# Weight conversion in an attention, FFT-mixing and gating kernel: temporaries moved to PSUM, the second weight's lower parts moved to VectorE

## The chip, the cores and the metric

The kernel runs on one core of a Trainium2 chip. The metric is the device time of one execution in microseconds (us). An engine takes its instructions in a fixed order; the engines are PE (TensorE: matmuls and transposes), DVE (VectorE), ACT (ScalarE), POOL (GpSimd) and SP (SyncE, which here only issues transfers). SBUF is the on-chip work memory, PSUM the smaller one into which PE writes; a full tile of it here is 128 partitions by 512 fp32 values, called a bank. GpSimd is given no operand in PSUM in this kernel.

## What is computed

The inputs are batches of 2, 8 heads, 768 positions, 64 values a head, all in fp32, and the weights, which come as fp64. Cut to what matters:

```
q_bucket, k_bucket = signs of q @ proj and k @ proj, as numbers     # 6 bits
scores = where(q_bucket == k_bucket, q @ k.T / 8, -1e9)
x = softmax(scores) @ v                          # [2, 768, 512] over all heads
u = x + real(fft(fft(x, axis=1), axis=2))
un = (u - mean(u)) / sqrt(var(u) + 1e-6)
y = u + relu(un @ w_ch1) @ w_ch2                 # 512 -> 2048 -> 512
gate = sigmoid(causal convolution of y over 5 positions)
out = (gate * (y @ w_val)) @ w_out
```

## The kernel before, in words

Matmuls run in fp16. Each operand is split into an upper part (its rounding to fp16) and a lower part (what is left), and a product is made of three matmuls: upper by upper, lower by upper, upper by lower. So every activation and every weight needs two elementwise steps, one for each part.

Weights are fp64 in device memory. `weights` (L414) loads a block into a ring of slots in SBUF and converts it in pieces. `widen` (L408) makes fp32 out of the two 32-bit halves by three instructions of VectorE: L410 (shift and mask of the high half into the temporary `wt`), L411 (sign and exponent bits, from ring and `wt` into `wt`), L412 (low bits, from ring and `wt` into `wt`). `split` (L128) then makes the two parts. Its last argument is a word of letters: with two letters, the first engine makes the upper part with the scale in the same instruction (`copy_of`, L112 on ScalarE) and the second the lower part, on VectorE by one instruction that scales and subtracts (`rest_of`, L126). With three letters, the first engine scales the temporary in place (L112 on ScalarE, L114 on GpSimd), the second makes the upper part and the third subtracts (L120). The words of the three sets of weights stand in `HOW`; a set with several words takes them in turn.

- First stretch, up to about 175 us: attention of batch 0 (`a0`), and beside it the first 1536 columns of `w_ch1`, 12 pieces of 128x512, word `av`. The temporaries are two buffers in the SBUF pool `tmp`. The loop at L953 steps through the attention's 38 remaining steps and makes one conversion after each step that `STEP` picks: before, every third (0, 3, 6 up to 33). `last` (L430) keeps a conversion's `widen` behind the newest score reduction on VectorE.
- Middle stretch, about 175 to 365 us: mixing of batch 0 (its FFT as matmuls, VectorE's sums on tile `z`), its norm, attention of batch 1 (`a1`) and the first feed-forward, and beside them the last 512 columns of `w_ch1` and all of `w_ch2`, 40 pieces of 128x256, word `aag`, temporaries in two buffers of the SBUF pool `wst`. `GATES` ties five of these pieces behind marks of other work.
- Late weights, 425 to 475 us: `w_val` and `w_out`, 8 pieces of 128x512, words `av`, `gag`, `av` in turn (three pieces with `gag`), temporaries in the SBUF pool `late`. Beside them runs the mixing of batch 1; after that the remaining feed-forwards and the gating, most of it PE.

The attention works in pairs of two score tiles (`pair`, L312): PE makes the scores (L320), VectorE their maximum (L330), ScalarE the exponential (L333) and the upper part (L112), GpSimd the lower part (L120), SyncE issues the transposing transfer (`at<-a`, L346), and PE multiplies by the values (`unit_out`, L355). `prep` (L230) splits q and k of the next group, transposes them (`tb<-st`, L247), and makes the hash products into a PSUM tile of the pool `pools.bt`, which has one buffer (L259), from which VectorE takes the signs (L264). Twice per `prep` that buffer is filled and read. Mixing's first matmuls (`zp`) and the norm's use the same pool.

All loads and transposes are issued by SyncE, in one order: a load that waits for its ring slot holds up the transposes behind it. The order of each engine's instructions is planned when the kernel is built, by a simulation of the instructions' times, which moves later work ahead into free places as far as data, buffers and the ties written by hand allow.

Of the kernel before, what the change touches and what calls it, by code (L numbers as in the profile page):

```python
# [9 lines left out]
INT32 = mybir.dt.int32  # L10
# [32 lines left out]
FLY = ('g', 'g')  # L43
CONV = "vvvv", "vvvv"
OO = ('aa', 'aa')
HOW = (('av',), ('aag',), ('av', 'gag', 'av'))
LEFT = 512
WB = 512
QW = {None: "s", "w2": "s"}
# [4 lines left out]
LO = {(1, 4, 0): 'v'}  # L54
NPRE = 0
PACE = 1
STEP = 3
W0 = 0
EARLY = (0, 'prep', 1)
UO = 'aa'  # L60
PREN = '-g'
# [16 lines left out]
def attention_fft_mix_gated_kernel(  # L78
# [49 lines left out]
    def split(h, l, i, s, how):  # L128

        unit = isinstance(s, float) and s == 1.0  # L130
        if len(how) == 3:
            if not unit:
                copy_of(i, i, s, how[0])
            s, unit, how = 1.0, True, how[1:]
        copy_of(h, i, s, how[0])
        if unit:
            return both(l, i, h, ALU.subtract, how[1])
        return rest_of(l, h, i, s, how[1])
# [18 lines left out]
    @contextmanager  # L157
    def after_mark(ins):
        with ExitStack() as stack:
            for i in ins:  # L160
                stack.enter_context(tc.issue_after(i))
            yield


    class Pool:
# [8 lines left out]
        def widen(self, stack, bufs):  # L174
            self.more, self.extra = stack.enter_context(tc.tile_pool(name="q_" + self.name, bufs=bufs, reuse_waits="tile", **self.kw)), bufs
            stack.callback(self.narrow)
# [237 lines left out]
    def weights(blocks, ring, pool, how, wp=WP, name=None, pre=()):  # L414

        n, m, at, rest = len(ring), len(pre), {}, list(enumerate(blocks))

        def load(done):
            while rest:
                i, (src, _, _, _) = rest[0]  # L420
                if i >= max(m, done) + n:
                    return
                at[i] = pre[i] if i < m else ring[(i - m) % n]
                nc.sync.dma_start(out=at[i], in_=src)
                rest.pop(0)

        load(0)
        yield
        for i, (src, h, l, s) in enumerate(blocks):
            r = at[i].rearrange("p (n x) -> p n x", x=2)  # L430
            for c in range(0, r.shape[1], wp):
                cl = slice(c, c + wp)
                t = pool.tile([128, wp], INT32, tag="wt", name="wt", bufs=2)
                k = (name, i * (r.shape[1] // wp) + c // wp)
                with after_mark([marks[GATES[k]]] if k in GATES else last if PACE and not name else []):
                    marks[k] = widen(t, r[:, cl, 0], r[:, cl, 1], t).ins
                split(h[:, cl], l[:, cl], t.bitcast(FP32), s, how[k[1] % len(how)])
                if cl.stop < r.shape[1]:
                    yield
            load(i + 1)  # L440
            yield

    def slots(t):
        return [t[:, i] for i in range(t.shape[1])]

    def w_blocks(src, dst, s, width, c0=0, c1=None):
        rows, cols = src.shape
        for c in range(c0, c1 or cols, width):
            for r in range(rows // 128):
                cl = slice(c, c + width)  # L450
                yield src[r * 128:(r + 1) * 128, cl].bitcast(INT32), dst[:, 0, r, cl], dst[:, 1, r, cl], s
# [425 lines left out]
    def drain(gen):  # L877
        for _ in gen:
            pass

    if True:
        base = ctx.enter_context(ExitStack())
        pools = AttnPools(base, ld=2, ta=2, tb=1, vt=2, e=2, a=3, at=2, sm=4, sc=2, pv=1, bt=1)
# [4 lines left out]
        tmp = att.enter_context(tc.tile_pool(name="tmp", reuse_waits="tile", bufs=1))  # L888
# [20 lines left out]
        wp = pools.pv.tile([128, 512], FP32, tag="pv", name="wp")  # L909
# [27 lines left out]
        with tc.issue_after(marks[EARLY]):  # L937
            nc.sync.dma_start(out=cf, in_=dft_f)
            nc.sync.dma_start(out=cs, in_=dft_s)
            nc.sync.dma_start(  # L940
                out=cwd.rearrange("p c j x -> p c (j x)"), in_=conv_t.bitcast(INT32).rearrange("(c p) j -> p c j", p=128)
            )
            w = weights(
                list(w_blocks(w_ch1, w1, W1S, WB, 0, DFF - LEFT)),
                slots(work.tile([128, 2048 // WB, 2 * WB], INT32, tag="big", name="ring")),
                tmp,
                HOW[0],
                W1P,
                pre=[work.tile([128, 4 * WP], INT32, tag="t4", name="pre", bufs=4) for _ in range(NPRE)],
            )  # L950
            next(w)
        widen(cw, cwd[:, :, :, 0], cwd[:, :, :, 1], cwt)
        for i, _ in enumerate(a0):  # L953
            if (i % STEP == W0 % STEP and i >= W0) if PACE else i % 4:
                next(w, None)
            if i in (A1LD, A1AT):
                next(a1)
        for _ in w:
            pass
        att.close()  # L960
        w2 = ctx.enter_context(tc.tile_pool(name="w2p", reuse_waits="tile", bufs=1)).tile([128, 2, NF, DM], FP16, name="w2")
        gen_p = ctx.enter_context(tc.tile_pool(name="gen", reuse_waits="tile", bufs=2, space=PSUM))
        wst = base.enter_context(tc.tile_pool(name="wst", reuse_waits="tile", bufs=1))
        w = weights(
            list(w_blocks(w_ch1, w1, W1S, WP, DFF - LEFT)) + list(w_blocks(w_ch2, w2, W2S, WP)), slots(wst.tile([128, 2, 2 * WP], INT32, name="ring2")), wst, HOW[1], name="w2"
        )
# [9 lines left out]
        if F0FIRST:  # L976
# [3 lines left out]
        late = ctx.enter_context(tc.tile_pool(name="late", bufs=1, side="right", reuse_waits="tile"))  # L980
        lps = ctx.enter_context(tc.tile_pool(name="lps", side="right", reuse_waits="tile", bufs=2, space=PSUM))
        lps2 = ctx.enter_context(tc.tile_pool(name="lps2", side="right", reuse_waits="tile", bufs=4, space=PSUM))
        wv = late.tile([128, 2, KC, DM], FP16, name="wv")
        wo = late.tile([128, 2, KC, DM], FP16, name="wo")
        w = weights(
            list(w_blocks(w_val, wv, WVS, DM)) + list(w_blocks(w_out, wo, WOS, DM)),
            [late.tile([128, 2 * DM], INT32, tag=t, name="ring3") for t in ("x2", "gt", "gv")],
            late,
            HOW[2],
            WLP,  # L990
        )
# [102 lines left out]
```

## Time and profile before

| what | value |
|---|---|
| median of 3 runs | 707.6 us (707.6 to 710.81) |
| the profiled execution | 703.61 us |
| its span, first to last instruction | 701.8 us |
| VectorE busy | 534.5 us (76%) |
| PE busy | 572.9 us (82%) |
| ScalarE busy | 350.9 us (50%) |
| GpSimd busy | 313.2 us (45%) |

The span is the time from the first to the last instruction on the core; the execution's own time is 1.8 us longer. In a group's row, L120 is a line of the kernel, then come engine, operation, out<-in by the program's tiles, shapes and count; behind the bar the busy time in us and the mean duration of one in ns, and behind the next bar how long the engine had stood idle just before, with what ended that. A queue's name carries a q (SPq). The granted clock (PEclk) is TensorE's, as a share of full speed.

### The profile page before, as it was taken

Reading aid. Unit: us, or ns where it says so; the run is one execution under the profiler, and the core shown is the slowest. Engines: PE = TensorE matmul, PEld = TensorE weight load, DVE = VectorE, ACT = ScalarE, POOL = GpSimd, SP = SyncE. Lnnn points to the kernel's source line nnn. Section 1 sums busy time; section 2 is a strip of 40 time slices with the busy share of each in tenths; the row PEclk is TensorE's granted clock in tenths of the full one; section 3 lists DMA queues with packets and bytes.
Section 4 is the critical chain, followed back from the end, with each engine's and each line's share of the span. In section 5 each row is a group of like instructions: output and inputs, shape, how many; then the busy total and the mean of one; then the engine's idle time right before and its main releaser. Section 6 shows DMA issues by size and latency. Waiting matters only on the chain.

```text
span 701.8 us, 12761 instructions
## 1 busy us (share of the span) xinstructions
PE 572.9 (82%) x4958; PEld 436.3 (62%) x4958; DVE 534.5 (76%) x1002; ACT 350.9 (50%) x731; POOL 313.2 (45%) x321
## 2 busy tenths in 40 slices
PE   5775576666664769988789999799989999999997
PEld 2334353444343547666567789678767788888864
DVE  5799797997999998999875629996799346182582
ACT  4576767883866445776578725321434302121142
POOL 5665959795577722876556431455232100000000
PEclk8557878868975799999989999999999999999999
DMA  3989999999578552676875884200000000000001
GB/s 118 203 233 222 238 236 223 215 221 204 139 151 179 135 144 65 146 165 148 163 133 109 157 159 151 91 1 2 0 31 31 32 1 1 1 2 1 1 31 61
DMA packets 191804, 79.72 MB, mean 114 GB/s; under 512 B 176384, under 2 KB 182144, under 8 KB 191744
## 3 DMA queue, kind: packets, MB, share of 16 engines
q1 hardware_dynamic: 191168, 78.81, 50.6%
q8 instruction: 39, 0.64, 0.4%
q10 hardware_dynamic: 576, 0.10, 0.1%
q14 instruction: 21, 0.17, 0.1%
HBM read 32.50 MB, written 3.15 MB: 51 GB/s over the span
## 4 chain that ended last, share of the span: by engine, by line
PE 33%; DVE 27%; DMA 6%; issue 5%; POOL 4%; ACT 2%; SPq 1%; ACTq 0%; DVEq 0%; POOLq 0%
PE f L720 12%; PE f L703 10%; DMA at<-a 3%; DVE wt L412 3%; PE pv L355 2%; DVE sc L330 2%; DVE wt L411 2%; DVE wt L410 2%; DVE gt L745 2%; PE op L864 2%; POOL a L120 2%; DVE z L120 2%; DMA ring<-in_moe_w_ch_dram 2%; DVE h L685 1%; PE vp L839 1%
## 5 line engine op out<-in xcount | busy, mean ns | idle before, releaser
L120 POOL TENSOR_TENSOR a<-e,a 128x384 f16<-128x384 f32 x184 | 183.5, 1021 | 90.6 <-ACT a L112 50.6
L703 PE MATMUL f<-un,w 128*128 128x256 f16 x1152 | 134.6, 274 | 5.0 <-DVE h L685 4.7
L720 PE MATMUL f<-h,w 128*128 128x256 f16 x1152 | 132.3, 273 | 0.9 <-POOL w L120 0.9
L703 PEld LDWEIGHTS <-w 128*128 128x128 f16 x1152 | 112.7, 98 | 24.0 <-issue 7.2
L720 PEld LDWEIGHTS <-w 128*128 128x128 f16 x1152 | 111.5, 98 | 16.2 <-POOL w L120 1.4
L355 PE MATMUL pv<-at,vt 128*64 128x256 f16 x864 | 77.7, 335 | 31.3 <-DMA at<-a 21.0
L330 DVE TENSOR_SCALAR_CACHE_REDUCE sc<-sc 128x768 f32<-128x768 f32 x96 | 91.4, 961 | 14.4 <-PE sc L320 13.2
L355 PEld LDWEIGHTS <-vt 128*64 128x64 f16 x864 | 62.0, 136 | 56.4 <-issue 38.7
L333 ACT ACTIVATE e<-sc,mx 128x768 f32<-128x768 f32 x96 | 85.5, 891 | 4.1 <-POOL a L120 1.2
L320 PE MATMUL sc<-ta 96*128 96x384 f16 x192 | 54.4, 367 | 39.0 <-ACT e L333 28.6
L112 ACT ACTIVATE a<-e 128x768 f16<-128x768 f32 x96 | 79.9, 839 | 11.1 <-DMA at<-a 7.9
L685 DVE SCALAR_TENSOR_TENSOR h<-f,h 128x512 f16<-128x512 f32 x48 | 32.6, 684 | 34.4 <-ACT h L684 34.2
L320 PE MATMUL sc<-tb 128*128 128x384 f16 x192 | 56.1, 376 | 0.0
L684 ACT ACTIVATE h<-f 128x512 f16<-128x512 f32 x48 | 28.4, 591 | 49.2 <-PE f L703 49.0
L320 PEld LDWEIGHTS <-ta 96*128 96x128 f16 x192 | 17.5, 103 | 56.3 <-issue 42.0
L120 POOL TENSOR_TENSOR w<-wt,w 128x256 f16<-128x256 f32 x40 | 36.1, 910 | 32.6 <-ACT w L112 32.4
L112 ACT ACTIVATE x<-xb 128x256 f16<-128x256 f32 x24 | 11.8, 534 | 67.3 <-DVE xb L691 66.9
L331 ACT ACTIVATE mx<-mx 128x1 f32<-128x1 f32 x96 | 18.8, 197 | 52.7 <-DVE sc L330 48.1
L412 DVE SCALAR_TENSOR_TENSOR wt<-ring,wt 128x256 int32<-128x256 int32 (+1 forms) x60 | 43.3, 728 | 0.4
L691 DVE SCALAR_TENSOR_TENSOR xb<-f,xb 128x256 f32<-128x256 f32 x24 | 13.7, 615 | 37.6 <-PE f L720 37.6
L411 DVE SCALAR_TENSOR_TENSOR wt<-ring,wt 128x256 int32<-128x256 int32 (+1 forms) x60 | 41.3, 696 | 0.5
L812 DVE SCALAR_TENSOR_TENSOR gt<-xb,cw,gt 128x256 f32<-128x256 f32 x60 | 37.1, 673 | 0.0
(144 smaller groups left out, 905.5 us busy)
## 6 DMA issues: line engine op xcount, KB each, us to landing
ring<-in_moe_w_ch_dram SPq DMA_DIRECT2D x40, 256.0 KB, 3.0
ring<-in_moe_w_ch_dram SPq DMA_DIRECT2D x12, 512.0 KB, 4.4
lv<-in_v_dram SPq DMA_DIRECT2D x8, 384.0 KB, 3.7
out_dram<-ob SPq DMA_DIRECT2D x12, 256.0 KB, 2.0
lq<-in_q_dram SPq DMA_DIRECT2D x7, 384.0 KB, 3.8
lk<-in_k_dram SPq DMA_DIRECT2D x7, 384.0 KB, 4.2
ring<-in_moe_w_val_dram SPq DMA_DIRECT2D x4, 512.0 KB, 4.2
ring<-in_moe_w_out_dram SPq DMA_DIRECT2D x4, 512.0 KB, 3.5
```

Of the source, the lines that this page charges most:

```text
L112: return nc.scalar.activation(out=o, in_=i, func=ACTF.Copy, scale=s)
L120: return (nc.gpsimd if eng == "g" else nc.vector).tensor_tensor(out=o, in0=i0, in1=i1, op=op)
L320: nc.tensor.matmul(out=s[:, n, 0:384], lhsT=z[0:rows, 0, hh, r], rhs=z[0:rows, 1, hh, n * 384:n * 384 + 384], start=(x == 0), stop=(x == 1),)
L330: last[:] = [nc.vector.tensor_scalar(s, s, -(PEN * PEN) / 2, None, ALU.max, ALU.max, accum_out=m[:, 0:1]).ins]
L333: marks["first", 2 + j] = nc.scalar.activation(out=e.rearrange("p (a b) -> p a b", a=2), in_=s, func=ACTF.Exp, bias=m[:, 1:2], scale=SC, a ...
L355: nc.tensor.matmul(out=p[64 * hh:64 * hh + 64, :], lhsT=va[g][:, hh, c, x, :], rhs=at[hh][:, :, y, c, :], start=(c == 0 and n == 0), stop= ...
L411: nc.vector.scalar_tensor_tensor(out=tmp, in0=hi, scalar=-0x40000000, in1=tmp, op0=ALU.bitwise_and, op1=ALU.bitwise_or)
L412: return nc.vector.scalar_tensor_tensor(out=dst, in0=lo, scalar=29, in1=tmp, op0=ALU.logical_shift_right, op1=ALU.bitwise_or)
L685: nc.vector.scalar_tensor_tensor(out=h[:, 1, f:f + 2, :], in0=p, scalar=0.0, in1=h[:, 0, f:f + 2, :], op0=ALU.max, op1=ALU.subtract)
L703: nc.tensor.matmul(out=p[:, o, :], lhsT=w1[:, i, kd, (f + o) * 128:(f + o) * 128 + 128], rhs=un[:, j, kd, :], start=(k == 0), stop=(k == 3 ...
L720: nc.tensor.matmul(out=p[:, o, :], lhsT=w2[:, i, f, (d + o) * 128:(d + o) * 128 + 128], rhs=h[:, j, f, :], start=(k == 0), stop=(k == 3 * ...
L812: nc.vector.scalar_tensor_tensor(out=o, in0=src, scalar=cw[:, d, j:j + 1].bitcast(FP32), in1=o, op0=ALU.mult, op1=ALU.add)
```

## The change

Four things change. (1) `HOW`: the 40 pieces of the middle stretch go from `aag` to `av`, so that ScalarE makes the upper part with the scale in one instruction and VectorE makes the lower part; the three late pieces with `gag` become `av` as well. (2) The temporary `wt` of the first stretch is a whole PSUM bank from `pools.bt`, the pool with one buffer that the hash products use; that of the late weights is a bank of `lps2`, with four buffers. The middle stretch keeps its two buffers in SBUF. (3) The pacing of the first stretch: the 12 conversions follow steps 0, 3, 6, 8, 11, 13, 16, 19, 21, 24, 26 and 29. (4) `drain(w)` stands for the loop that did the same.

```diff
--- before.py
+++ after.py
@@ -43,7 +43,7 @@
 FLY = ('g', 'g')
 CONV = "vvvv", "vvvv"
 OO = ('aa', 'aa')
-HOW = (('av',), ('aag',), ('av', 'gag', 'av'))
+HOW = (('av',), ('av',), ('av',))
 LEFT = 512
 WB = 512
 QW = {None: "s", "w2": "s"}
@@ -54,8 +54,7 @@
 LO = {(1, 4, 0): 'v'}
 NPRE = 0
 PACE = 1
-STEP = 3
-W0 = 0
+STEP = 31
 EARLY = (0, 'prep', 1)
 UO = 'aa'
 PREN = '-g'
@@ -430,7 +429,7 @@
             r = at[i].rearrange("p (n x) -> p n x", x=2)
             for c in range(0, r.shape[1], wp):
                 cl = slice(c, c + wp)
-                t = pool.tile([128, wp], INT32, tag="wt", name="wt", bufs=2)
+                t = pool.tile([128, 512], INT32, tag="g", name="wt")[:, 0:wp] if name != "w2" else pool.tile([128, wp], INT32, tag="wt", name="wt", bufs=2)
                 k = (name, i * (r.shape[1] // wp) + c // wp)
                 with after_mark([marks[GATES[k]]] if k in GATES else last if PACE and not name else []):
                     marks[k] = widen(t, r[:, cl, 0], r[:, cl, 1], t).ins
@@ -943,7 +942,7 @@
             w = weights(
                 list(w_blocks(w_ch1, w1, W1S, WB, 0, DFF - LEFT)),
                 slots(work.tile([128, 2048 // WB, 2 * WB], INT32, tag="big", name="ring")),
-                tmp,
+                pools.bt,
                 HOW[0],
                 W1P,
                 pre=[work.tile([128, 4 * WP], INT32, tag="t4", name="pre", bufs=4) for _ in range(NPRE)],
@@ -951,12 +950,11 @@
             next(w)
         widen(cw, cwd[:, :, :, 0], cwd[:, :, :, 1], cwt)
         for i, _ in enumerate(a0):
-            if (i % STEP == W0 % STEP and i >= W0) if PACE else i % 4:
+            if i * 12 // STEP != (i - 1) * 12 // STEP and i < STEP:
                 next(w, None)
             if i in (A1LD, A1AT):
                 next(a1)
-        for _ in w:
-            pass
+        drain(w)
         att.close()
         w2 = ctx.enter_context(tc.tile_pool(name="w2p", reuse_waits="tile", bufs=1)).tile([128, 2, NF, DM], FP16, name="w2")
         gen_p = ctx.enter_context(tc.tile_pool(name="gen", reuse_waits="tile", bufs=2, space=PSUM))
@@ -985,7 +983,7 @@
         w = weights(
             list(w_blocks(w_val, wv, WVS, DM)) + list(w_blocks(w_out, wo, WOS, DM)),
             [late.tile([128, 2 * DM], INT32, tag=t, name="ring3") for t in ("x2", "gt", "gv")],
-            late,
+            lps2,
             HOW[2],
             WLP,
         )
```

## Rows read from the trace of the kernel before

**Rows 1.** Windows, length, busy PE, PEld, DVE, ACT, POOL, PEclk, DMA share, GB/s
```profile
50.00:175.00 125.00, 81.30 (x715) 54.92 (x715) 109.05 (x174) 87.98 (x189) 91.92 (x86) 0.79 1.09 221
175.00:350.00 175.00, 128.50 (x1131) 93.62 (x1128) 163.54 (x319) 107.83 (x240) 108.79 (x112) 0.88 0.63 143
350.00:425.00 75.00, 69.85 (x678) 56.46 (x677) 40.51 (x81) 47.76 (x104) 34.23 (x38) 0.95 0.76 150
425.00:475.00 50.00, 43.66 (x432) 38.37 (x430) 48.15 (x95) 19.88 (x28) 19.36 (x19) 1.00 0.19 62
475.00:700.00 225.00, 217.42 (x1875) 179.43 (x1872) 136.59 (x273) 60.05 (x113) 27.34 (x20) 1.00 0.04 15
```

**Rows 2.** Timeline of SyncE's queue, 30 to 180 us: start, duration
```profile
35.51 9.82 SPq L346 DMA_TRANSPOSE at<-a  x1
50.05 0.33 SPq L424 DMA_DIRECT2D ring<-in_moe_w_ch_dram  x1
...
160.90 12.31 SPq L346 DMA_TRANSPOSE at<-a  x3
173.26 1.05 SPq L424 DMA_DIRECT2D ring<-in_moe_w_ch_dram  x2
```

**Rows 3.** Timeline of VectorE, 43 to 54 us
```profile
43.42 1.02 DVE L410 TENSOR_SCALAR wt<-ring 128x512 int32<-128x512 int32 x1
...
46.05 0.42 DVE L410 TENSOR_SCALAR wt<-ring 128x512 int32<-128x512 int32 x1
46.39 0.68 DVE L411 SCALAR_TENSOR_TENSOR wt<-ring,wt 128x512 int32<-128x512 int32 x1
...
48.62 1.40 DVE L412 SCALAR_TENSOR_TENSOR wt<-ring,wt 128x512 int32<-128x512 int32 x1
...
52.30 1.22 DVE L126 SCALAR_TENSOR_TENSOR w<-wt,w 128x512 f16<-128x512 f32 x1
```

**Rows 4.** VectorE by form, 40 to 160 us: busy, mean ns, idle
```profile
L412 DVE SCALAR_TENSOR_TENSOR wt<-ring,wt 128x512 int32<-128x512 int32 x12 | 12.9, 1073 | 0.1
L126 DVE SCALAR_TENSOR_TENSOR w<-wt,w 128x512 f16<-128x512 f32 x12 | 12.7, 1067 | 2.0 <-ACT w L112 2.0
L411 DVE SCALAR_TENSOR_TENSOR wt<-ring,wt 128x512 int32<-128x512 int32 x12 | 12.0, 1000 | 0.1
L410 DVE TENSOR_SCALAR wt<-ring 128x512 int32<-128x512 int32 x12 | 7.9, 654 | 0.1
```

**Rows 5.** Groups of VectorE by form, 175 to 365 us
```profile
L412 DVE SCALAR_TENSOR_TENSOR wt<-ring,wt 128x256 int32<-128x256 int32 x40 | 24.6, 625 | 0.3
L411 DVE SCALAR_TENSOR_TENSOR wt<-ring,wt 128x256 int32<-128x256 int32 x40 | 23.9, 606 | 0.3
L410 DVE TENSOR_SCALAR wt<-ring 128x256 int32<-128x256 int32 x40 | 19.3, 486 | 3.7 <-DMA ring<-in_moe_w_ch_dram 3.0 <-POOL w L120 0.6
...
L685 DVE SCALAR_TENSOR_TENSOR h<-f,h 128x512 f16<-128x512 f32 x8 | 5.5, 683 | 0.4 <-ACT h L684 0.3
```

**Rows 6.** Tile wt, 40 to 160 us: min/median/max ns, starts
```profile
L126 DVE SCALAR_TENSOR_TENSOR w<-wt,w x12: 679/1146/1400, 52.3 to 151.4; 128x512 f16<-128x512 f32 x12
```

**Rows 7.** Tile wt, 175 to 365 us
```profile
L410 DVE TENSOR_SCALAR wt<-ring x40: 275/294/1709, 176.3 to 352.8; 128x256 int32<-128x256 int32 x40
...
L412 DVE SCALAR_TENSOR_TENSOR wt<-ring,wt x40: 390/421/1137, 179.0 to 357.6; 128x256 int32<-128x256 int32 x40
...
L120 POOL TENSOR_TENSOR w<-wt,w x40: 662/672/5902, 185.0 to 362.4; 128x256 f16<-128x256 f32 x40
```

**Rows 8.** Groups of GpSimd by form, 175 to 350 us
```profile
L120 POOL TENSOR_TENSOR w<-wt,w 128x256 f16<-128x256 f32 x38 | 34.7, 923 | 30.2 <-ACT w L112 30.1
```

**Rows 9.** Waits of SyncE's queue, 175 to 350 us: total, times, longest
```profile
SPq L346 <- POOL w L120: 30.8, 9, 4.0
```

**Rows 10.** Tile wt, 425 to 475 us
```profile
L410 DVE TENSOR_SCALAR wt<-ring x8: 408/420/833, 427.1 to 455.5; 128x512 int32<-128x512 int32 x8
...
L126 DVE SCALAR_TENSOR_TENSOR wv<-wt,wv x3: 683/690/1130, 434.4 to 443.1; 128x512 f16<-128x512 f32 x3
```

## The prediction

> **What bounds the kernel now.** I read the stretches first, then the queue that issues the transfers, then the groups of VectorE and GpSimd in each stretch. The rows to look at are those in which one column fills the stretch [rows 1].
>
> From 50 to 175 us it is the transfers. VectorE works 109 of 125 us, GpSimd 92, ScalarE 88, PE 81, and the sixteen DMA engines show a share of 1.09 [rows 1]. The queue itself shows why: SyncE issues one transfer behind the other, a transpose holding it for some 4 us (three in 12.31), until the first load for the next stage at 173.26 [rows 2]; 25 transposes and 17 plain loads follow each other there with at most half a microsecond between two. The one hole is at the start: the issue begun at 35.51 ends at 45.33, the next load goes at 50.05, and the VectorE instruction that frees its slot, L412 begun at 48.62 for 1.40 us, ends at 50.02 [rows 2, 3].
>
> From 175 to 350 us it is VectorE: 163.5 of 175 us busy, PE 128.5, ScalarE 107.8, GpSimd 108.8 [rows 1]. Mixing of batch 0, attention of batch 1 and forty conversions of weights share that engine. From 350 us on PE is short of nothing for long (69.9 of 75, 43.7 of 50, 217.4 of 225), so what comes late at 350 comes late at the end; only from 425 to 475 is VectorE full too (48.2 of 50) [rows 1].
>
> One property of the rows carries the argument. A VectorE instruction with two inputs in SBUF has no fixed price. L412 on 128x512 takes 1073 ns on the mean in the first stretch [rows 4] and can take 680 (one of the interleaved ones did in about that: L411 at 46.39, 0.68 us) [rows 3]. L685, which takes one input from PSUM and one from SBUF at the same size, has a mean of 683 ns in the middle of a stretch where GpSimd is 62% busy [rows 1, 5]. So what stretches the first kind and leaves the second alone goes with GpSimd's reading of SBUF.
>
> **First stretch: temporaries in PSUM, one buffer, new pacing.** Twelve conversions of 128x512 cost VectorE 654 + 1000 + 1073 + 1067 = 3794 ns each, 45.5 us [rows 4]. After the change L411, L412 and L126 read the temporary from PSUM; I price them like L685, 683 ns [rows 5]. L410 writes PSUM; no row shows that form. Bounds: 0.42 us, its quickest in this program [rows 3], and 0.68 us, the price of L685 at the same size. I take 0.68. Sum 4 x 0.68 = 2.73, 12 x 2.73 = 32.8 us, so VectorE works 12.7 us less.
>
> The Trainium skill, VectorE: DVE Perf Modes, section Why PSUM operands drop a tier, speaks against the change here: an operand in PSUM takes the two-port rate from such an instruction. By it L410 goes to the upper bound, by the row of before it would stay at the lower; the sum differs by 12 x 0.26 = 3 us of VectorE's time, which is hidden either way.
>
> Of the 12.7 us nearly nothing reaches the end: VectorE has 16 us free in this stretch as it is [rows 1], and SyncE's queue covers it [rows 2]. What can be gained is the hole of 4.7 us. With one buffer the second conversion can't be woven into the first, so its L410 (0.42) and L411 (0.68) no longer stand ahead of the first one's L412, which itself falls from 1.40 to 0.68, and its L410 from 1.02 [rows 3]: 0.42 + 0.68 + 0.72 + 0.34 = 2.2 us. I take **-2 us** (ends -4.7 and, if the single buffer holds things up, +8, see below). The new pacing moves conversions by at most four steps. The last one began its L126 at 151.4 us [rows 6], and the queue sets the stretch's end at 173: nothing, covered by the queue. Without that cover the same VectorE work would only stand elsewhere in the stretch, and its worst is one conversion, 2.7 us, in front of something urgent.
>
> **Middle stretch: VectorE takes over the lower parts.** Per conversion, 40 times: one ScalarE scaling goes (ScalarE is 62% busy, off the path, nothing), one GpSimd subtraction goes, median 672 ns, mean 923 [rows 7, 8], and one VectorE L126 on 128x256 comes, with both inputs in SBUF (this temporary is not moved to PSUM). Its nearest rows are L412 and L411 of the same size and stretch: median 421 ns, the undisturbed price, and mean 625 [rows 5, 7]. GpSimd is busy 62% of the stretch; without the 34.7 us of these subtractions [rows 8] 108.8 - 34.7 = 74 of 175, 42%. If the surcharge of 204 ns shrinks with that share, the new instruction costs 421 + 204 x 42/62 = 559 ns, 40 x 559 = 22.4 us (ends 16.8 and 25.0).
>
> The same shrinking gives time back. L412: (625 - 421) x 20/62 = 66 ns; L411: (606 - 421) x 20/62 = 60; L410: (486 - 294) x 20/62 = 62; together 188 ns x 40 = 7.5 us [rows 5, 7] (for L411 the median of L412, the form being the same). For the fewer other instructions with two inputs in SBUF I allow 1.5. Net on VectorE: 22.4 - 9 = +13.4 us, in a stretch where it has 11.5 idle [rows 1]. Those holes are where data were late; a longer queue fills some of them. I let half of them absorb: **+8 us** (ends: -6, if GpSimd's instructions cost VectorE their whole length, see below, and +16, nothing absorbed and the dear price).
>
> SyncE's transposes wait 30.8 us in this stretch for a GpSimd `w` [rows 9]. That wait goes, but the engine that makes their data is full, so the next wait is for the same conversions' L412 or for the scores on VectorE. Nothing; at most 3 us. Behind each new L126 stands everything else of VectorE's queue, the score reductions of attention 1 first, and ScalarE's exponentials wait for those; L126 also waits for ScalarE's upper part. Twelve such in the first stretch lost 2.0 us in all, 0.17 each [rows 4]; at that rate 40 lose 6.7, which is within the upper end.
>
> **Late weights.** Eight conversions of 128x512. Their temporaries in PSUM cost L410 the step from 0.42 to 0.68, 8 x 0.26 = 2.1 us [rows 10]; three more L126 at 0.69, 2.1 us [rows 10]; L411 and L412 I leave as they are. GpSimd loses three scalings and three subtractions, so that the dear L126 (up to 1.13 us) [rows 10] becomes 0.68 and the mixing beside it loses some surcharge; at the 0.2 us an instruction of the middle stretch I allow 2 us for both. VectorE +2, PE has matmuls of the feed-forward beside it: **0** (-3 to +3).
>
> **Sum.** -2 + 8 + 0 = +6 us. The profiled execution took 703.6 us (span 701.8, 1.8 around it), 4 below the median of 707.6. Against the median: **713.6 us**. About half a per cent, 3.5 us, is what a measurement of this kernel can tell from no change.
>
> **Rivals.** *GpSimd's instructions cost VectorE their whole length* (faster). If each of the 40 subtractions stops VectorE for its own 672 ns [rows 7], 26.9 us come free against 16.8 added at the undisturbed price: VectorE -10, with the same share of absorption -6, with the first stretch's -2 the time is 699.6. The Trainium skill, SBUF — State Buffer, section Who interferes with whom, has this rule: the pair of ports shared by the two engines is locked, and the loser stands still for the whole instruction. By that rule, taken at its full length, this rival is the forecast. For it: L410 on 128x256 has reached 1709 ns against a median of 294, GpSimd's own 5902 against 672 [rows 7]. Against it: half of all L410 and L412 run at their floor though GpSimd is busy 62% of the time, and the mean surcharge is only 0.2 us. It decides once the surcharge that leaves VectorE is over 0.42 us per subtraction taken away; my shares give 0.23. 28%.
>
> *The extra work is covered* (no change). The last subtraction begins at 362.4 us [rows 7], and VectorE has 34 us free from 350 to 425 [rows 1]. If the second half of the weight slips there without keeping PE waiting, +13 costs at most 2: 707 to 709. Against it: PE's filler work there needs exactly that weight. 14%.
>
> *The single PSUM buffer holds up the preparation* (slower still). One conversion holds its temporary from 43.42 to 53.5 us, 10 us [rows 3], and the same buffer takes each group's hash products, on PE's queue ahead of the scores. Three groups are prepared in this stretch; three waits of half a conversion are 15 us at worst, and as the transfer queue covers part of each I take 8 on top of the forecast: 722. It decides once a preparation waits for longer than its transpose would have stood in the queue. Against it: the order is planned with the buffer known. 15%.
>
> **How the numbers follow.** Forecast 43%, the rivals 28, 14 and 15. Of the forecast's 43, 36 lie over 711, 5 within half a per cent, 2 below; of the first rival's 28, 27 are faster; of the cover's 14, 13 are no change; of the buffer's 15, 12 are slower. That gives faster 0.30, same 0.22, slower 0.48. The range takes in the first rival with a little more gain in the hole, 697, and the buffer rival with the middle stretch's upper end, 727. The likeliest case alone would be 705 to 722.
>
> **What would show it.** Right: L126 on 128x256 forty times at 0.5 to 0.6 us; L411 and L412 of 128x512 at 0.68 in the first stretch; SyncE's queue still full from 50 to about 171; VectorE busy over 165 us in the middle, and the stretch in which PE is short ending some 6 us later. Wrong: L410 to L412 of 128x256 falling to their floor together with the attention's GpSimd work (first rival), PE gaps ahead of L259 (third), or the first stretch ending much before 168, which would mean that it was not the transfers that held it.

## The result, and the profile after

The changed kernel takes 714.8 us (median of 4 runs, 713.05 to 719.94); its ratio to the kernel before is 1.0113, 95% interval 1.008 to 1.0146. The profiled execution took 713.05 us with a span of 711.3, so the two profiles differ by 9.5 us, the medians by 7.2. Every line behind 57 stands one lower in the changed kernel (L410 is L409, L126 is L125, L346 is L345). Variants made from the kernel before keep its numbers.

Windows of the changed kernel, with the columns and stretches of [rows 1]:

```profile
50.00:175.00 125.00, 82.98 (x683) 56.53 (x686) 95.32 (x171) 90.48 (x199) 85.82 (x90) 0.73 1.11 222
175.00:350.00 175.00, 129.37 (x1146) 93.46 (x1135) 165.86 (x336) 89.71 (x186) 73.22 (x70) 0.88 0.59 131
350.00:425.00 75.00, 69.72 (x676) 55.75 (x674) 39.71 (x81) 51.07 (x111) 35.70 (x40) 1.00 0.67 116
425.00:475.00 50.00, 47.74 (x472) 42.45 (x470) 40.58 (x86) 18.92 (x27) 5.74 (x9) 1.00 0.39 118
475.00:700.00 225.00, 211.43 (x1826) 176.15 (x1824) 149.22 (x285) 59.25 (x110) 32.59 (x24) 0.98 0.03 12
```

Against [rows 1], VectorE has 13.7 us less to do from 50 to 175 us and 2.3 more from 175 to 350; GpSimd loses 35.6 there. Up to 475 us PE has done no less than before. It falls behind after that, by 6 us, in a stretch that none of the change's instructions touches. The marks of these profiles are to be read with care: the profiled execution of the kernel before (703.61 us) was 3 to 4 us quicker than its medians.

VectorE by form, 40 to 160 us (as [rows 4]; those of the twelve that begin in it):

```profile
L409 DVE TENSOR_SCALAR wt<-ring 128x512 int32<-128x512 int32 x11 | 7.7, 704 | 0.2
L410 DVE SCALAR_TENSOR_TENSOR wt<-ring,wt 128x512 int32<-128x512 int32 x10 | 7.2, 719 | 0.1
L411 DVE SCALAR_TENSOR_TENSOR wt<-ring,wt 128x512 int32<-128x512 int32 x10 | 7.1, 710 | 0.1
L125 DVE SCALAR_TENSOR_TENSOR w<-wt,w 128x512 f16<-128x512 f32 x10 | 6.9, 685 | 7.5 <-ACT w L111 7.5
```

All four stand near 0.7 us where three of them had a mean of 1.0 or more [rows 4].

Timeline of SyncE's queue in the changed kernel, 0 to 195 us (as [rows 2]):

```profile
3.95 0.94 SPq L423 DMA_DIRECT2D ring<-in_moe_w_ch_dram  x2
...
13.59 8.67 SPq L423 DMA_DIRECT2D ring<-in_moe_w_ch_dram  x3
...
30.72 3.77 SPq L246 DMA_TRANSPOSE tb<-st  x1
...
42.38 8.39 SPq L345 DMA_TRANSPOSE at<-a  x1
51.47 0.33 SPq L423 DMA_DIRECT2D ring<-in_moe_w_ch_dram  x1
51.89 8.45 SPq L345 DMA_TRANSPOSE at<-a  x2
...
157.10 17.82 SPq L345 DMA_TRANSPOSE at<-a  x4
```

A row's second number is the stretch from the start of its first issue to the end of its last, with waits in between. Two things are to be seen. The hole of 4.7 us at 45 us [rows 2] is gone, as planned. But loads of the **second** weight now go from 3.95 us on (6 of them before 23 us; before, the first went at 173.26 [rows 2]), and the three from 13.59 us on are spread over 8.67 us: each issue takes 0.33 us, and between them the queue stands, for VectorE's `wt` above all. With the temporary out of the pool `tmp`, the second weight's ring no longer shares its memory with attention 0, and the plan pulls six conversions into the first 30 us. The first `tb<-st` starts at 30.72 instead of 27.1 us, and the last transpose of the stretch ends at 157.10 + 17.82 = 174.92 us instead of 173.21.

VectorE by form, 175 to 365 us (as [rows 5]; 34 pieces, the other six being the early ones), and the waits of SyncE's queue, 175 to 350 us (as [rows 9]), with one row of the kernel before behind them:

```profile
L411 DVE SCALAR_TENSOR_TENSOR wt<-ring,wt 128x256 int32<-128x256 int32 x34 | 19.3, 579 | 0.2
L125 DVE SCALAR_TENSOR_TENSOR w<-wt,w 128x256 f16<-128x256 f32 x34 | 19.3, 582 | 0.9 <-ACT w L111 0.6
L410 DVE SCALAR_TENSOR_TENSOR wt<-ring,wt 128x256 int32<-128x256 int32 x34 | 19.2, 572 | 0.2
L409 DVE TENSOR_SCALAR wt<-ring 128x256 int32<-128x256 int32 x34 | 16.3, 490 | 3.0 <-DMA ring<-in_moe_w_ch_dram 3.0
```

```profile
SPq L423 <- DVE wt L411: 29.1, 11, 5.0
SPq L345 <- POOL a L119: 17.2, 6, 5.6
SPq L423 <- DVE z L510: 15.0, 2, 14.6
```

```profile
SPq L424 <- DVE wt L412: 42.1, 20, 5.5
```

L125 has a mean of 582 ns. The queue's wait for GpSimd's `w` is gone. Its loads wait for VectorE's `wt` less long than before (29.1 us on this row, 42.1 before), and its transposes wait longer for GpSimd's `a` (17.2 us, 9.3 before).

Windows of the changed kernel where PE falls behind, same columns:

```profile
480.00:490.00 10.00, 8.58 (x89) 7.52 (x88) 10.00 (x24) 1.37 (x2) 1.67 (x3) 1.00 0.01 2
490.00:500.00 10.00, 4.90 (x57) 4.01 (x57) 10.00 (x13) 2.31 (x5) 9.39 (x6) 1.00 0.01 2
500.00:510.00 10.00, 9.81 (x88) 7.84 (x87) 9.83 (x26) 3.51 (x10) 0.00 (x0) 0.83 0.00 0
510.00:520.00 10.00, 6.61 (x51) 4.34 (x49) 10.00 (x24) 3.62 (x8) 2.49 (x1) 1.00 0.15 54
520.00:530.00 10.00, 8.88 (x44) 6.25 (x45) 7.04 (x17) 3.11 (x9) 4.83 (x4) 0.66 0.00 1
530.00:540.00 10.00, 8.50 (x62) 6.12 (x61) 9.96 (x22) 3.39 (x6) 1.32 (x1) 1.00 0.14 52
```

VectorE is full and PE stands; and after PE has stood (4.90 of 10 busy, 6.61 of 10) the granted clock of the next ten us is 0.83 and 0.66, a mean in which part of the ten us stands at the lower of the two levels, 1.2 GHz, and the rest at 2.4. Groups of PE, 475 to 550 us, of the changed kernel:

```profile
L760 PE MATMUL vp<-x,wv 128*128 128x256 f16 x144 | 19.7, 296 | 3.5 <-DVE x L125 3.2 <-ACT ob L774 0.3
...
L591 PE MATMUL mp<-cs,r 128*128 128x128 f16 x72 | 5.5, 235 | 2.3 <-DVE xb L599 2.3
L647 PE MATMUL var<-mean_w,sq 128*128 128x1 f32 x16 | 2.8, 297 | 4.5 <-POOL sq L119 4.5
```

and of the kernel before:

```profile
L761 PE MATMUL vp<-x,wv 128*128 128x256 f16 x144 | 17.3, 272 | 2.3 <-DVE gt L752 1.6 <-DVE xb L691 0.6
L592 PE MATMUL mp<-cs,r 128*128 128x128 f16 x50 | 3.4, 219 | 0.0
```

PE now waits for batch 1: for its mixing (`xb`, `mp`) and its norm (`sq`). Attention 1 ends 13 us later, mixing and norm follow it, and the feed-forwards of batch 0, with which PE had bridged this before, are finished *earlier* (489.9 against 498.2 us). The second weight was ready earlier too (last lower part done at 353.8 against 363.1). The fourth feed-forward (ffn 3, the first of batch 1) starts at 536.8 instead of 508.2 us. From its end on both kernels are alike. The same 144 `vp` matmuls keep PE busy for 19.7 instead of 17.3 us, 2.4 us more, in a stretch of which part was granted the lower clock.

### The profile page after: what moved, and what is told of

Same layout as the page of the kernel before. It is cut to its first block, busy times and chain, and to the rows that moved or that the text cites. A ratio compares the mean times of both kernels' runs of the same rounds, so it can differ in the third digit from the quotient of the medians.

```text
span 711.3 us, 12670 instructions
## 1 busy us (share of the span) xinstructions
PE 574.8 (81%) x4958; PEld 439.5 (62%) x4958; DVE 536.8 (75%) x1045; ACT 338.2 (48%) x691; POOL 260.7 (37%) x275
## 5 line engine op out<-in xcount | busy, mean ns | idle before, releaser
L119 POOL TENSOR_TENSOR a<-e,a 128x384 f16<-128x384 f32 x184 | 172.6, 963 | 155.3 <-ACT a L111 96.2
L719 PE MATMUL f<-h,w 128*128 128x256 f16 x1152 | 133.8, 276 | 0.2 <-DVE w L125 0.2
L111 ACT ACTIVATE w<-wt 128x256 f16<-128x256 f32 (+1 forms) x52 | 23.1, 454 | 41.5 <-DVE wt L411 41.2
L690 DVE SCALAR_TENSOR_TENSOR xb<-f,xb 128x256 f32<-128x256 f32 x24 | 13.7, 614 | 36.1 <-PE f L719 36.1
L125 DVE SCALAR_TENSOR_TENSOR w<-wt,w 128x256 f16<-128x256 f32 (+1 forms) x52 | 30.7, 603 | 10.5 <-ACT w L111 9.9
L410 DVE SCALAR_TENSOR_TENSOR wt<-ring,wt 128x256 int32<-128x256 int32 (+1 forms) x60 | 38.1, 642 | 0.3
## 6 DMA issues: line engine op xcount, KB each, us to landing
ring<-in_moe_w_ch_dram SPq DMA_DIRECT2D x12, 512.0 KB, 4.2
ring<-in_moe_w_val_dram SPq DMA_DIRECT2D x4, 512.0 KB, 4.3
ring<-in_moe_w_out_dram SPq DMA_DIRECT2D x4, 512.0 KB, 3.5
```

The source lines that it names most:

```text
L111: return nc.scalar.activation(out=o, in_=i, func=ACTF.Copy, scale=s)
L119: return (nc.gpsimd if eng == "g" else nc.vector).tensor_tensor(out=o, in0=i0, in1=i1, op=op)
L125: return nc.vector.scalar_tensor_tensor(out=l, in0=i, scalar=s, in1=h, op0=ALU.mult, op1=ALU.subtract)
L410: nc.vector.scalar_tensor_tensor(out=tmp, in0=hi, scalar=-0x40000000, in1=tmp, op0=ALU.bitwise_and, op1=ALU.bitwise_or)
L719: nc.tensor.matmul(out=p[:, o, :], lhsT=w2[:, i, f, (d + o) * 128:(d + o) * 128 + 128], rhs=h[:, j, f, :], start=(k == 0), stop=(k == 3 * ...
```

## The experiments

Three theories at the start. **A**: VectorE's 40 added instructions delay attention 1. **B**: the single PSUM buffer holds up batch 1's preparation. **C**: the six conversions pulled to the front delay attention 0. All variants compute the whole reference. The table gives for each the median, its ratio to the kernel before, and from its profile the end of attention 1's last unit (last `pv<-at` matmul), the start of ffn 3, and PE's busy time and granted clock from 475 to 550 us.

| kernel | us | ratio, interval | attention 1 ends | ffn 3 starts | PE busy of 75, clock |
|---|---|---|---|---|---|
| before | 706.9 | | 420.5 | 508.2 | 70.4, 1.00 |
| changed | 714.8 | 1.0113, 1.008 to 1.0146 | 433.3 | 536.8 | 62.3, 0.93 |
| middle undone (u_mid) | 707.5 | 1.001, 0.9994 to 1.0026 | 427.4 | 515.3 | 70.4, 1.00 |
| first stretch's temporaries undone (u_first) | 711.5 | 1.0067, 1.0043 to 1.0091 | 431.0 | 531.3 | 64.9, 0.95 |
| late undone (u_late) | 722.2 | 1.0199, 1.0158 to 1.024 | 436.8 | 540.4 | 58.8, 0.91 |
| no early conversions (u_nohoist) | 716.9 | 1.0147, 1.0131 to 1.0163 | 439.6 | 537.1 | 66.5, 0.95 |
| before + middle (d_mid) | 722.4 | 1.0223, 1.0205 to 1.0241 | 436.7 | 540.2 | 59.7, 0.89 |
| before + half of middle (d_half) | 725.2 | 1.0256, 1.0243 to 1.027 | 436.7 | 533.7 | 58.9, 0.93 |
| before + first stretch (d_first31) | 715.9 | 1.0112, 1.0085 to 1.014 | 429.1 | 518.6 | 69.6, 0.95 |
| before + pacing (d_step) | 709.5 | 1.0034, 1.0021 to 1.0046 | 428.6 | 520.7 | 68.4, 0.98 |
| before + late (d_late) | 706.4 | 0.9998, 0.9983 to 1.0013 | 425.7 | 516.3 | 68.7, 0.98 |
| changed + tie (u_tie) | 707.3 | 0.9999, 0.998 to 1.0017 | 426.5 | 516.5 | 68.2, 1.00 |
| before + middle + tie (dm_tie) | 718.3 | 1.0154, 1.0121 to 1.0186 | 430.9 | 514.9 | 69.0, 0.98 |
| before + tie (d_tie) | 717.5 | 1.013, 1.0089 to 1.0171 | 428.0 | 512.0 | 71.5, 1.00 |

A mark of one profile is good to some five us, and the marks don't order the times. The edit of d_late bears on nothing before 425 us, and yet its first feed-forward starts at 263.9 instead of 260.9 us, and its attention 1 ends 5.2 us later than before at the same median. U_first ends attention 1 at 431.0 with 711.5 us, d_first31 at 429.1 with 715.9.

**The middle stretch alone and undone.** d_mid against before, u_mid against the changed kernel:

```diff
# d_mid
-HOW = (('av',), ('aag',), ('av', 'gag', 'av'))
+HOW = (('av',), ('av',), ('av', 'gag', 'av'))
# u_mid
-HOW = (('av',), ('av',), ('av',))
+HOW = (('av',), ('aag',), ('av',))
```

> The kernel before with only the middle stretch changed (av instead of aag, 40 lower parts on VectorE, temporaries in SBUF as before). A: 40 x 0.56 added, some 9 us given back by GpSimd's silence, half absorbed: 713 to 717 us, VectorE's L126 on 128x256 at 0.55 to 0.60 us. B and C: 707 to 709, nothing to hold up and nothing pulled ahead.

> The changed kernel with the middle stretch's lower parts back on GpSimd (aag); the first stretch's PSUM temporaries and pacing and the late weights stay as changed. A, VectorE's extra load in the middle stretch delays batch 1's attention: most of the loss goes, 705 to 709 us, the last unit of batch 1's attention (PE pv) ends near 421 us as before instead of 433. B, the single PSUM buffer holds up batch 1's preparation: stays at 713 to 716, first score reduction of batch 1 still near 186 us and last unit near 432. C, the conversions pulled to the first 30 us: stays at 713 to 716 too, since they are pulled ahead here as well.

Alone it costs 15.4 us, and taking it out of the changed kernel gives back 7.3, all but 0.6 of the loss. Attention 1's end went with it only in part: it comes at 427.4 us, where I had expected about 421. VectorE by form, 175 to 365 us, in d_mid:

```profile
L126 DVE SCALAR_TENSOR_TENSOR w<-wt,w 128x256 f16<-128x256 f32 x40 | 23.9, 604 | 1.0 <-ACT w L112 0.6
L412 DVE SCALAR_TENSOR_TENSOR wt<-ring,wt 128x256 int32<-128x256 int32 x40 | 21.8, 555 | 0.2
L411 DVE SCALAR_TENSOR_TENSOR wt<-ring,wt 128x256 int32<-128x256 int32 x40 | 21.2, 536 | 0.1
L410 DVE TENSOR_SCALAR wt<-ring 128x256 int32<-128x256 int32 x40 | 17.2, 434 | 2.9 <-DMA ring<-in_moe_w_ch_dram 2.8
```

Against [rows 5] the three old instructions give back 2.8 + 2.7 + 2.1 = 7.6 us, 0.19 us for each subtraction taken from GpSimd. For these three that leaves a net addition of 23.9 - 7.6 = 16.3 us. Over the whole execution VectorE is busy for 548.0 us in d_mid and 534.5 before, so all its other instructions gave back 10.4 us, 0.26 for each subtraction, and the net addition is 13.5. The time grows by 15.4: nothing of it was absorbed.

**Half of it.**

```diff
-HOW = (('av',), ('aag',), ('av', 'gag', 'av'))
+HOW = (('av',), ('aag', 'av'), ('av', 'gag', 'av'))
```

> The kernel before with every second piece of the middle stretch as av (20 lower parts on VectorE, 20 on GpSimd). If the loss grows with VectorE's added time: half of the 15.4 us of all forty, 713 to 717. If a few holes of VectorE absorb the first part: 707 to 711. If it is the switch itself (the plan's order with two engines instead of three): 719 to 723.

Half the pieces on VectorE cost more than all of them (725.2). That is outside all three of the ranges above, and a price for each added instruction can't say it. Nor is the sum of VectorE's work a better guide: over the whole execution it is 548.4 us here, as in d_mid (548.0). Attention 1 ends at 436.7 us in both. That the planned order is what they have in common is a guess at this point.

**The first stretch.** d_first31 puts temporaries and pacing into the kernel before, d_step the pacing alone, u_first takes the PSUM temporaries of that stretch out of the changed kernel. The temporaries with the old pacing weren't tried.

```diff
# d_step, d_first31
-            if (i % STEP == W0 % STEP and i >= W0) if PACE else i % 4:
+            if i * 12 // 31 != (i - 1) * 12 // 31 and i < 31:
# d_first31; u_first has the reverse in the changed kernel
...
-                tmp,
+                pools.bt,
...
```

> The kernel before with only the new pacing of the first stretch (12 conversions by step 29, temporaries in SBUF). If the pacing is hidden by the transfer queue, as the prediction said: 706 to 709. If the earlier end of the conversions clears VectorE for batch 1's preparation: 700 to 704, with the first score reduction of batch 1 near 170 us, as in the changed kernel with SBUF temporaries (169.9), where it was 175.9 before.

> The kernel before with the first stretch's temporaries in the one PSUM buffer and the new pacing, which such temporaries need; middle stretch and late weights as before. If the changed kernel's loss is the middle stretch's alone: 706 to 709, as with the middle undone (707.5). If PSUM temporaries cost by the single buffer (batch 1's first score reduction some 10 us late): 709 to 714.

> The changed kernel with the first stretch's temporaries back in the two SBUF buffers (pacing, middle stretch and late weights as changed). With them the second weight's ring lies again over memory of the attention, so its first loads go at about 173 us instead of 4. A: the loss stays, 712 to 717 us. B: most of it goes, 705 to 709, first score reduction of batch 1 back near 176 us. C: most of it goes, 705 to 709, while the first pair of scores is back at 27 us instead of 34.

The pacing, which I had costed at nothing, costs 2.6 us, and with the temporaries the stretch costs 9.0; undone in the changed kernel they give back 3.3. Theory B's wait is there: VectorE takes the signs of batch 1's first group (`ta<-bt`) at 175.7 us, behind a conversion that holds the buffer up to 172.9, and before at 158.4; the first score of attention 1 comes at 186.0 instead of 175.9. But u_first, which starts attention 1 at 169.9, ends it at 431.0, hardly before the changed kernel's 433.3. The late start is made good (the third unit of attention 1 ends at 248.4 against 246.7). So the late start isn't where the time goes, and yet part of the time goes with the temporaries: 6.4 us in the kernel before (715.9 against d_step's 709.5), 3.3 in the changed one (714.8 against 711.5). Whether it is the one buffer that costs this isn't shown, and the 9.0 us of d_first31, above both its ranges, have no place yet: PE falls behind there mostly from 350 to 425 us (65.6 us busy, 69.9 before), but so it does in u_mid (65.0), at 707.5 us. VectorE has some 5 us less to do in d_first31 than before (529.2 against 534.5 us).

**No early conversions.** Two idle tiles in `tmp` take the place of the old temporaries:

```diff
+        hold = [tmp.tile([128, 512], INT32, tag="wt", name="hold", bufs=2) for _ in range(2)]
+        for t in hold:
+            nc.vector.memset(t[:, 0:1], 0)
```

> The changed kernel with 4 KB per partition of the attention's SBUF pool held by two idle tiles, so that the second weight's ring can't be loaded before that pool is given up: the six conversions of the first 30 us go back to the middle stretch, PSUM temporaries stay. A: VectorE gets 6 conversions more in the middle, 6 x 2.2 = 13 us: 715 to 725. B: no change, 713 to 716. C: 705 to 709.

The early loads are gone and the time isn't better (716.9): theory C falls. The 2.1 us by which it is worse lie within the two intervals. Against u_first, which has no early loads either and its temporaries in SBUF, it is 5.4 us worse (716.9 and 711.5; the two idle tiles differ too), which is again a price of the temporaries in PSUM.

**The late weights.**

```diff
# d_late, in the kernel before; u_late is the reverse in the changed kernel
-HOW = (('av',), ('aag',), ('av', 'gag', 'av'))
+HOW = (('av',), ('aag',), ('av',))
...
-            late,
+            lps2,
...
```

> The kernel before with only the late weights changed (av throughout, temporaries in four PSUM buffers). If the late weights' surcharge on VectorE from 425 to 475 us is on the path: 702 to 705 us, VectorE's busy time there falls from 48 of 50 us. If PE's filler covers that stretch, as the prediction said: 706 to 708.

> The changed kernel with the late weights as before (SBUF temporaries, three pieces with `gag`). If the late part is worth nothing, as alone (706.4 against 706.9): 713 to 716. If it gives back what it gave beside the first part (715.9 with the first part alone, 707.5 with first and late), the time without it is 719 to 724.

Alone it is worth nothing (706.4). In the changed kernel it is worth 7.4 us, and beside the first stretch 8.4 (715.9 against u_mid's 707.5). Windows of u_late and of u_mid, 475 to 550 us:

```profile
475.00:550.00 75.00, 58.81 (x494) 46.49 (x493) 70.46 (x135) 18.86 (x41) 25.43 (x19) 0.91 0.02 8
```

```profile
475.00:550.00 75.00, 70.42 (x642) 57.96 (x640) 63.34 (x148) 24.57 (x55) 29.65 (x19) 1.00 0.04 15
```

In u_late the gating's `vp` matmuls begin at 509.5 us, in the changed kernel at 489.7, in both directly behind batch 0's last feed-forward (509.7 and 489.9), so with the late part these are finished earlier and PE comes to the gating while batch 1 is in its norm. Why they end earlier isn't shown. GpSimd's share of mixing 1 goes down with it (`z`, 8 instructions: median 962 ns in u_late, 645 in the changed kernel). Which of the late part's two edits does this wasn't separated.

**The order.** By then a fourth theory stood: VectorE's work isn't too much, but is planned in a bad order. The conversions are written ahead of attention 1, so, it says, the plan gives them VectorE first, and attention 1 pays. From 240 to 350 us conversions (tile `wt`) keep VectorE busy for 47.9 us in the changed kernel and 40.7 before, and 14 of attention 1's scores are reduced there against 16. Windows of tile `wt`, before (VectorE, ScalarE, GpSimd) and changed (VectorE, ScalarE), busy us each, then the clock and the DMA's share and rate:

```profile
240.00:310.00 70.00, 23.86 (x54) 13.88 (x36) 13.96 (x19) 0.98 0.48 119
310.00:350.00 40.00, 16.82 (x26) 7.43 (x18) 7.12 (x9) 1.00 0.78 159
240.00:310.00 70.00, 27.95 (x57) 5.36 (x15) 0.96 0.43 102
310.00:350.00 40.00, 19.95 (x37) 3.80 (x10) 0.89 0.79 173
```

The test ties the last 26 pieces behind the newest score reduction:

```diff
-                with after_mark([marks[GATES[k]]] if k in GATES else last if PACE and not name else []):
+                with after_mark([marks[GATES[k]]] if k in GATES else last if PACE and (not name or free[0] < 0) else []):
...
+    free = [0]
...
-        drain(w)
...
-        drain(a1)
+        for _ in range(14):
+            next(w, None)
+        free[0] = -1
+        for _ in a1:
+            next(w, None)
+        drain(w)
+        free[0] = 0
```

> The changed kernel with the same tie. Theory O: attention 1's last unit ends by about 425 instead of 433.3 us, time 707 to 711. Rival W: 713 to 716. Third case (second weight late): over 717.

> The kernel before with `av` in the middle stretch (722.35 us) and, on top, the last 26 pieces of the second weight each tied behind the newest score reduction of attention 1, so that VectorE alternates between a conversion and a score. Theory O (the plan gives the conversions VectorE first, and attention 1 pays): attention 1's last unit ends by about 425 instead of 436.7 us, and the time falls to 707 to 714. Rival W (VectorE is full there, and the sum of its work decides): 719 to 724, with the unit's end where it was. Third case (conversions now so late that PE waits for the second weight): over 725, with PE idle ahead of the feed-forward before 425 us.

> The kernel before with the same tie: the control. Both theories: its order of conversions and scores was nearly this one already, so 705 to 709. Over 711 would mean that the tie itself costs something; below 704 that it helps whatever the conversions' engine.

Windows of u_tie:

```profile
350.00:425.00 75.00, 68.87 (x622) 51.53 (x624) 44.67 (x89) 50.34 (x112) 36.90 (x40) 0.91 0.70 131
475.00:550.00 75.00, 68.23 (x622) 56.01 (x620) 67.22 (x148) 24.77 (x55) 26.32 (x19) 1.00 0.04 15
```

In the changed kernel the tie gives back the whole loss (714.8 to 707.3) with every one of VectorE's instructions still there. Rival W (the sum of the work decides) falls for this kernel: with another order the same work costs nothing. D_first31 and u_nohoist say the same, with some 5 us less for VectorE than before and a loss of 9.0 and 10.0 us. Conversions slip into the free stretch from 350 us on (VectorE 44.7 us busy instead of 39.7), attention 1 ends 6.8 us earlier, PE is kept busy to 550 us, and from 475 us on its clock stays at full.

That an order costs and another doesn't is shown; that attention 1 waits for conversions on VectorE is not. The result of each unit of attention 1 is taken up by VectorE (`xb<-pv`). Those from 340 to 440 us, the sixth to the twelfth unit, first and last start behind the three durations, in the kernel before, the changed kernel, u_mid and u_tie:

```profile
L371 DVE TENSOR_TENSOR xb<-pv,xb x7: 423/606/625, 351.4 to 421.4; 128x256 f32<-128x256 f32 x7
L370 DVE TENSOR_TENSOR xb<-pv,xb x7: 423/611/621, 354.5 to 434.2; 128x256 f32<-128x256 f32 x7
L370 DVE TENSOR_TENSOR xb<-pv,xb x7: 394/604/624, 356.5 to 428.2; 128x256 f32<-128x256 f32 x7
L370 DVE TENSOR_TENSOR xb<-pv,xb x7: 417/611/625, 347.3 to 427.4; 128x256 f32<-128x256 f32 x7
```

At the sixth unit the changed kernel is 3.1 us behind the kernel before, and 2.0 us ahead of u_mid. The other 9.7 us come behind it, after the last conversion (353.8 us), where VectorE is busy for 26.3 of the 55 us to 425. One thing that differs there is PE's order: matmuls of the feed-forwards (tile `f`) from 350 to 370 us, in the same four kernels (PE, VectorE, ScalarE, then the clock and the DMA's share and rate):

```profile
350.00:370.00 20.00, 6.37 (x55) 0.00 (x0) 0.00 (x0) 0.83 0.77 143
350.00:370.00 20.00, 12.63 (x104) 2.51 (x4) 1.16 (x2) 1.00 0.44 80
350.00:370.00 20.00, 4.10 (x33) 0.00 (x0) 0.00 (x0) 0.83 0.72 140
350.00:370.00 20.00, 4.20 (x18) 0.00 (x0) 0.00 (x0) 0.66 0.50 113
```

So there is a rival that no run here tests: the second weight is ready earlier, batch 0's feed-forward goes ahead of attention 1 on PE, and is then missing as work for PE behind 490 us. A run that ties the feed-forwards behind attention 1 and leaves the conversions alone would tell the two apart.

The control shows the limits of that. In the kernel before the same tie costs 10.6 us where I had expected nothing, and d_mid with it (718.3) falls between the two theories. Groups of PE in d_tie, 350 to 425 us:

```profile
L355 PE MATMUL pv<-at,vt 128*64 128x256 f16 x181 | 14.4, 303 | 9.9 <-DMA at<-a 9.9
L722 PE MATMUL f<-h,w 128*128 128x256 f16 x99 | 13.1, 283 | 1.1 <-ACT w L112 0.8 <-POOL w L120 0.4
```

and in the kernel before:

```profile
L355 PE MATMUL pv<-at,vt 128*64 128x256 f16 x216 | 16.5, 298 | 4.7 <-DMA at<-a 4.6
```

In d_tie PE waits 9.9 us for transposes, 5.2 more than before, and 1.2 us for the second weight, whose last pieces come 8 us later (371.1 against 363.1). That is the third case of dm_tie's and u_tie's expectations, in small part only; the profile is of the quickest of d_tie's executions (713.75 us), and where the rest of its 10.6 us lies isn't shown. So an order that suits one kernel hurts its neighbour. Which order is right for d_mid stays open, and nothing here is measurably faster than the kernel before.

## Why the prediction came out as it did

713.6 us was predicted and 714.8 came, on the predicted side and in the predicted stretch. The sum is better than its terms, and that is luck: three of them are off by 7 to 11 us, with opposite signs.

- **Prices of instructions.** First stretch: 683 ns predicted for the forms with PSUM, 685 to 719 measured; VectorE 12.7 us less predicted, 13.7 measured. L410 went to the upper bound: 682 ns median in the late stretch into PSUM, 420 into SBUF [rows 10]. This agrees with the Trainium skill, VectorE: DVE Perf Modes, section Why PSUM operands drop a tier. Middle: 559 ns predicted for the new L126, 582 measured (604 in d_mid); 7.5 us given back by the three old instructions predicted, 7.6 measured in d_mid, against the profile before. In the changed kernel the profiles of u_mid and the changed kernel put it at 4.0 us for 34 pieces (118 ns for the three together), 0.12 us for each subtraction.
- **First rival** (GpSimd's instructions cost VectorE their whole length). It needed over 0.42 us back for each subtraction; 0.19 came on the three instructions, 0.26 on all of VectorE's. The Trainium skill, SBUF — State Buffer, section Who interferes with whom, taken at the full length of the instruction, differs here from the measurement.
- **First stretch, -2 us.** Failed; in the kernel before, the stretch's two edits cost 9.0 us. The hole closed and the stretch ended no earlier: the last transpose ends at 174.9 us, without the early loads at 173.8 (u_nohoist), before at 173.2, and in d_late, where this stretch is untouched, at 174.6. I also hadn't asked who gets the memory that `wt` leaves. "Nothing" for the pacing was wrong too: 2.6 us alone.
- **Middle stretch, +8 us, half absorbed.** Alone it is +15.4, with nothing absorbed. VectorE's idle time in the stretch was no cover. I had let half of the addition vanish in it without a row that shows this. With another order of the same instructions nothing is lost (u_tie, 707.3), so neither a full price nor a half one is a property of the added instructions. The forecast also lacked PE's part: its order from 350 us on, its waiting between 490 and 530 us, and the fallen clock.
- **Late weights, 0.** Right alone; in the changed kernel -7.4 us. Alone the three parts come to 15.4 + 9.0 - 0.5 = 23.9 us, together to 7.9. Of the 16 us between, 9.1 lie between the middle and the first stretch, which together cost 15.3 (u_late, 722.2) instead of 24.4, and 6.9 lie in the late part. No run shows how either comes about. That is how a sum with terms too low came out right.
- **The cover rival** is refuted as it stood: the second weight didn't slip behind 350 us, it was finished 9 us earlier. With the tie, which makes it slip, the rival's 707 to 709 is what is measured (707.3).
- **The buffer rival** had its later start (17 us at `ta<-bt`), and that was made good. But the temporaries in PSUM cost 3.3 us in the changed kernel and 6.4 in the one before; by what, isn't shown, so this rival is not refuted at a lower price than its 8 us.

## What to carry to other kernels

Don't price an added instruction by the idle time of its stretch: here 13.5 us of added work cost 15.4 alone, and nothing in another order. Ask what the new order moves on the other engines too, and test the order by itself, with the same instructions. Ask of every buffer that is moved who takes its old memory, and what that lets start early. Parts that are worth nothing alone can be worth 1% together, so undo parts in the changed kernel as well as adding them to the old one.

## What the runs showed of the hardware that was not expected

- The forms with one PSUM operand had little spread beside a busy GpSimd: in the first stretch of the changed kernel, with GpSimd busy for 86 of 125 us, L409 to L411 and L125 take 667 to 751 ns; before, with SBUF operands, L411, L412 and L126 take 655 to 2128.
- A wait of PE was paid twice here: in the changed kernel the ten us after a half idle stretch (4.90 of 10) were granted 0.83 of full speed, and the ten after 6.61 of 10 0.66. The 144 `vp` matmuls from 475 to 550 us kept PE busy for 19.7 us instead of 17.3.
- Taking 40 GpSimd subtractions with a median of 0.67 us each out of the middle stretch gave VectorE's other instructions 0.26 us back for each (d_mid).
